# The reciprocals of the softmax sums take a way through DRAM instead of TensorE, and the gated products start a step later

## The chip, the core and the metric

The kernel runs on one core of a Trainium2 chip. A time is the device time of one execution in microseconds. Of the kernel before there are three runs, with the median 1103.42 us (1102.9 to 1108.34), and one profiled execution. In the profile PE is TensorE's matmul stream, DVE is VectorE, ACT is ScalarE, POOL is GpSimd, and SP is SyncE, which here issues nearly all DMAs.

## What is computed

An attention with a threshold, a gated feed-forward network and a second feed-forward network, all in float32:

```python
scores = scale * q @ k.T                              # 4 batches, 8 heads, 576 tokens, 64 wide
scores = where(scores >= max(scores) - tau, scores, -1e9)
attn = exp(scores - max(scores))
attn = attn / (attn.sum(-1) + 1e-9)
x = (attn @ v)                                        # heads side by side: 2304 tokens x 512
h = ((x @ w1) * (x @ w2)) @ w3 @ w_out                # 1024 wide inside
out = leaky_relu(h @ w_in, 0.01) @ w_out2             # 2048 wide inside
```

The change concerns the division by the sum: one factor for each query of each head.

## The kernel before

**Units and steps.** A unit is a pair of heads and one of two groups of queries. There are 32. Group 0 has 256 queries, in two chunks of 128 (a "two-chunk unit", two steps); group 1 has 320, in a chunk of 64 queries that carries both heads side by side on the partitions (`None` in the code) and two chunks of 128 (a "three-chunk unit", three steps). For each batch the four pairs of group 0 come first and then the four of group 1, so four two-chunk units (8 steps) and four three-chunk units (12 steps) alternate, and there are 80 steps.

**One step.** In step n the loop (lines 455 to 516 of before) masks chunk n, issues the scores of chunk n + 1, transposes the masked exponentials of chunk n, and in the first step of a unit multiplies the unit before with its values (`weighted`, tile `av`, copied to `xs`). Scores (`sc`, L219; L215 for the `None` chunk) stand in one PSUM tile with a single buffer. VectorE takes the maximum of each head (`nm`, L225), ScalarE the exponential (`e`, L227), and VectorE masks it and sums it (L241). In the last step of a unit VectorE also scales the next unit's queries (`qk`, L199), and for a three-chunk unit copies the 64-query part, scaled, into a block-diagonal tile `qz` (L194), which the next L215 reads.

**The sums.** VectorE makes the reciprocals `rr` (L305, L306), one row per query on 128 partitions. The heads' outputs `xs` have queries along the free axis and 64 partitions per head, so each reciprocal is needed on 64 partitions. Before, GpSimd spreads it (`rb`, L308 and L313), TensorE transposes it into PSUM (`bc`, L324; L322 for the chunk of 64), and VectorE multiplies (L325). This is `normalise`. ScalarE and GpSimd then split the product into two parts, `x`.

**The filler.** When the four units of a group are done, their `x` go through the gated network (`gated`): 24 pieces of 12 matmuls each (tiles `psab`, L383, and `psh`, L402), which the loop deals out between the scores and the transposes of the next group's steps. How many a step gets follows from a running sum: rate 1.22 or 1.55 times the step's weight (1 for the `None` chunk, 2 for others), rounded down, the rest carried on; a step's pieces stand at three places. Until the first gated pass the filler is the product of two weight matrices (`fold_weights`, L361), whose operands ScalarE, VectorE and GpSimd decode from 64-bit words (L142 to L153).

**What sets the order.** PE's order in the attention is the order of the code (`manual_schedule`). SyncE's too, until the second gated pass begins; after that, and on the other engines, a scheduler sets it, except that instructions marked `keep_in_program_order` keep their order among each other. `av`, `bc`, `psab`, `psh` and the fold share two PSUM buffers (tag `w`).

Of the kernel before, what the change touches and what calls it, by code (L numbers as in the profile page):

```python
# [8 lines left out]
F32 = mybir.dt.float32  # L9
# [4 lines left out]
ALU = mybir.AluOpType  # L14
# [3 lines left out]
P = 128  # L18
B, H, S, D = 4, 8, 576, 64
# [9 lines left out]
Q0 = (0, 128, 320, 448)  # L29
GROUPS = ((0, 256, (0, 1)), (HF, 320, (2, 3)))  # L30
NK = 5
CHUNKS = ((0, 1), (None, 2, 3))
STEPS = tuple(
    (b * 4 + p, g, c) for b in range(B) for g in range(2) for p in range(4) for c in CHUNKS[g])
# [5 lines left out]
def attention_gated_ffn(ctx: ExitStack, tc: tile.TileContext, qkv, tau, w3t, wout, w12, w2, out):  # L40
# [6 lines left out]
    nc = tc.nc  # L47
# [8 lines left out]
    h3d = tc.dram_tile([KD, P, NT], F32, name="h3d")  # L56

# [10 lines left out]
    pairs = cpool.tile([P, D], F32, name="pairs")  # L68
    nc.vector.tensor_tensor(out=pairs, in0=ident[:, :D], in1=ident[:, D:], op=ALU.add)
    sides = cpool.tile([P, P], F32, name="sides")  # L70
    nc.vector.memset(sides, 0.0)
    nc.vector.memset(sides[:D, :D], 1.0)
    nc.vector.memset(sides[D:, D:], 1.0)
# [4 lines left out]
    one = cpool.tile([P, 1], F32, name="one")  # L78
    nc.vector.memset(one, 1.0)
# [220 lines left out]
    def reciprocals(pair, g):  # L300

        st = stat.pop((pair, g))
        n = 4 + g
        rr = apool.tile([P, 5], F32, tag="rr", name="rr", bufs=2)
        nc.vector.tensor_scalar(out=rr[:, :n], in0=st[:, :n], scalar1=1e-9, scalar2=None, op0=ALU.add)  # L305
        nc.vector.reciprocal(rr[:, :n], rr[:, :n])  # L306
        rb = apool.tile([P, 3, P], F32, tag="rb", name="rb")
        nc.gpsimd.tensor_tensor(  # L308
            out=rb[:, :2].rearrange("p c (h d) -> p (c h) d", h=2),
            in0=rr[:, :4].unsqueeze(2).to_broadcast([P, 4, D]),  # L310
            in1=one.unsqueeze(2).to_broadcast([P, 4, D]), op=ALU.mult)
        if g:
            nc.gpsimd.tensor_tensor(  # L313
                out=rb[:, 2], in0=rr[:, 4:5].to_broadcast([P, P]), in1=sides, op=ALU.mult)
        rb_t[pair, g] = rb

    def normalise(pair, g):
        gq, gw, cs = GROUPS[g]
        xs, rb = xs_t.pop((pair, g)), rb_t.pop((pair, g))
        bc = ps_w.tile([P, 512], F32, tag="w", name="bc")  # L320
        if g:
            nc.tensor.matmul(bc[:, :D], rb[:, 2], pairs, start=True, stop=True)  # L322
        for i, c in enumerate(cs):
            nc.tensor.transpose(bc[:, Q0[c] - gq:Q0[c] - gq + P], rb[:, i], ident)  # L324
        nc.vector.tensor_tensor(out=xs[:, :gw], in0=xs[:, :gw], in1=bc[:, :gw], op=ALU.mult)  # L325
        x = xpool.tile([P, 2, 320], F32R, tag="x", name="x")
        nc.scalar.copy(x[:, 0, :gw], xs[:, :gw])
        nc.gpsimd.tensor_tensor(
            out=x[:, 1, :gw], in0=xs[:, :gw], in1=f(x[:, 0, :gw]), op=ALU.subtract)
        x_t[pair, g] = x  # L330
# [106 lines left out]
    def run(gen, k):  # L437
        for _ in range(k):
            if next(gen, 0) == 0:
                return  # L440
# [10 lines left out]
    weigh, norm = [], []  # L451
# [3 lines left out]
    for n in range(NS):  # L455
# [30 lines left out]
        if norm:  # L486
            normalise(*norm.pop())
        if last_of_unit:
            reciprocals(pair, g)
            weigh.append((pair, g))  # L490
        elif u and STEPS[n - 1][:2] != (pair, g):
            norm.append(units[u - 1])
        fill(2)
        if n == 0 or STEPS[n - 1][:2] != (pair, g):
            load_unit(u + 2)
        load_halves(kh - kh // 2)
        if last_of_unit and pair % 4 == 3:
            queue.append((n + 2, pair // 4, g))
# [18 lines left out]
    weighted(*weigh.pop())  # L517
    run(filler, 2)
# [140 lines left out]
```

## Time and profile before

| | us |
|---|---|
| median of three runs | 1103.42 |
| profiled execution | 1105.57 |
| its span, first to last instruction | 1103.8 |
| PE busy | 1054.0 |
| VectorE busy | 508.8 |
| ScalarE busy | 473.5 |
| GpSimd busy | 256.6 |

The span is 1.77 us shorter than the execution that it is from, and that execution 2.15 us longer than the median. Attention fills the first 650 us, the rest is the second network. "Granted clock" is TensorE's clock as a share of 2.4 GHz; its lower level, 0.50, is 1.2 GHz. A matmul's own duration in the profile includes its way through the array, so that neighbours overlap: what one adds is read from the starts.

### The profile page before, as it was taken

To read this page: it belongs to the slowest core of one execution; us is meant where nothing else is said; L and a number is where in the kernel's file an instruction comes from. 1 tells how busy PE (TensorE), PEld (TensorE's weight loads), DVE (VectorE), ACT (ScalarE), POOL (GpSimd) and SP (SyncE) were. 2 spreads that over 40 slices of the span, in tenths; PEclk is the share of its full clock that TensorE was granted. 3 is DMA by queue.
4 is the path that set the end of the run, shared out by engine and by line. 5 is a ranking of instruction groups with operands and counts; after the bars stand their busy time and mean duration, and the time that the engine had idled before them with its cause. 6 is when DMAs were issued, how large, how long until landed. Compare 5 with 4: busy or idle time off the path is not lost.

```text
span 1103.8 us, 16025 instructions
## 1 busy us (share of the span) xinstructions
PE 1054.0 (95%) x6288; PEld 852.2 (77%) x6288; DVE 508.8 (46%) x1087; ACT 473.5 (43%) x891; POOL 256.6 (23%) x256
## 2 busy tenths in 40 slices
PE   4799799999999999999999999999999999999998
PEld 2455478788877798887888789877888888888887
DVE  5666767555665555675546633365311211111111
ACT  4667744343444343543434443477422222222232
POOL 2436812021120111120212136477400100000000
PEclk8899899999999999999999999999999999999999
DMA  9563720311112111112120023356200010010010
GB/s 306 185 210 117 211 59 19 85 30 58 53 35 66 50 41 54 55 38 66 34 65 25 1 77 116 101 191 197 71 18 1 31 37 1 3 45 1 1 39 20
DMA packets 35098, 77.57 MB, mean 70 GB/s; under 512 B 4560, under 2 KB 19408, under 8 KB 32976
## 3 DMA queue, kind: packets, MB, share of 16 engines
q1 hardware_dynamic: 34880, 76.56, 22.0%
q8 instruction: 49, 0.80, 0.3%
q14 instruction: 25, 0.20, 0.1%
q10 hardware_dynamic: 144, 0.00, 0.0%
HBM read 67.11 MB, written 9.44 MB: 69 GB/s over the span
## 4 chain that ended last, share of the span: by engine, by line
PE 81%; DVE 7%; ACT 6%; DMA 2%; issue 2%; POOL 1%; ACTq 0%; SPq 0%; DVEq 0%; POOLq 0%
PE psab L383 16%; PE po L596 16%; PE ps L574 16%; PE psh L402 9%; PE av L294 7%; PE sc L219 6%; PE tp L272 4%; PE ps L361 4%; DVE e L241 2%; DVE t L145 1%; ACT t L142 1%; ACT e L227 1%; PE tq L277 1%; ACT HH L276 1%; ACT lw L144 1%
## 5 line engine op out<-in xcount | busy, mean ns | idle before, releaser
L383 PE MATMUL psab<-x,w 128*128 128x256 f32 (+1 forms) x1536 | 234.2, 303 | 2.7 <-DVE xs L325 2.0
L383 PEld LDWEIGHTS psab<-x,w 128*128 128x128 f32 x1536 | 208.9, 189 | 24.3 <-issue 16.0
L574 PE MATMUL ps<-h,w 128*128 128x512 f32 (+1 forms) x960 | 215.7, 370 | 0.6 <-DVE h L550 0.3
L596 PE MATMUL po<-w,gg 128*128 128x512 f32 x864 | 213.7, 392 | 1.8 <-ACT gg L581 1.8
L574 PEld LDWEIGHTS ps<-h,w 128*128 128x128 f32 x960 | 169.0, 188 | 36.5 <-POOL w L153 1.3
L596 PEld LDWEIGHTS po<-w,gg 128*128 128x128 f32 x864 | 159.3, 188 | 38.0 <-ACT gg L581 3.1
L582 DVE TENSOR_TENSOR gg<-gf,gg 128x512 fp32r<-128x512 f32 (+1 forms) x80 | 61.2, 765 | 269.9 <-ACT gg L581 268.2
L225 DVE TENSOR_REDUCE nm<-sc 128x1 f32<-128x576 f32 x144 | 108.8, 756 | 109.2 <-PE sc L219 67.0
L227 ACT ACTIVATE e<-sc,nm 128x576 f32<-128x576 f32 x144 | 107.0, 743 | 121.0 <-DVE nm L225 120.8
L579 ACT ACTIVATE gf<-ps 128x512 f32<-128x512 f32 (+1 forms) x80 | 44.3, 555 | 226.9 <-PE ps L574 226.9
L241 DVE SCALAR_TENSOR_TENSOR e<-sc,th,e 128x576 f32<-128x576 f32 x144 | 112.6, 815 | 45.9 <-ACT e L227 45.9
L402 PE MATMUL psh<-gt,w 128*128 128x256 f32 (+1 forms) x768 | 115.1, 301 | 0.6 <-ACT ht L409 0.5
L394 POOL TENSOR_TENSOR gt<-at,gt 128x256 fp32r<-128x256 f32 (+1 forms) x64 | 52.7, 824 | 262.9 <-ACT gt L393 262.9
L402 PEld LDWEIGHTS psh<-gt,w 128*128 128x128 f32 x768 | 104.1, 189 | 7.7 <-issue 5.4
L219 PE MATMUL sc<-qk 64*128 64x288 f32 x512 | 84.7, 451 | 24.5 <-DVE e L241 15.7
L272 PE MATMUL tp<-ident,e 128*128 128x128 f32 x512 | 78.7, 277 | 9.0 <-ACT HH L276 9.0
L219 PEld LDWEIGHTS sc<-qk 64*128 64x128 f32 x512 | 46.7, 196 | 44.4 <-issue 12.6
L272 PEld LDWEIGHTS tp<-ident,e 128*128 128x128 f32 x512 | 61.5, 142 | 19.4 <-ACT HH L276 11.5
L151 POOL TENSOR_TENSOR lw<-t,lw 128x512 int32<-128x512 int32 x48 | 65.8, 1375 | 26.7 <-ACT lw L144 14.8
L294 PE MATMUL av<-HH,vv 128*64 128x256 f32 (+1 forms) x512 | 69.7, 415 | 0.0
L551 POOL TENSOR_TENSOR h<-hr,h 128x1024 fp32r<-128x1024 f32 (+1 forms) x10 | 23.8, 2380 | 188.1 <-DVE h L550 188.1
L361 PE MATMUL ps<-wo,w 128*128 128x512 f32 x128 | 60.9, 621 | 6.2 <-DVE xs L325 4.7
(70 smaller groups left out, 961.1 us busy)
## 6 DMA issues: line engine op xcount, KB each, us to landing
st<-in_w SPq DMA_DIRECT2D x40, 512.0 KB, 4.5
vv<-in_qkv SPq DMA_DIRECT2D x64, 160.0 KB, 2.4
raw<-in_w3t SPq DMA_DIRECT2D x8, 1024.0 KB, 5.6
qk<-in_qkv SPq DMA_DIRECT2D x32, 208.0 KB, 3.5
qk<-in_qkv SPq DMA_DIRECT2D x32, 144.0 KB, 2.8
out<-os SPq DMA_DIRECT2D x18, 256.0 KB, 2.2
raw<-in_wout SPq DMA_DIRECT2D x4, 1024.0 KB, 10.0
raw<-in_w SPq DMA_DIRECT2D x4, 1024.0 KB, 6.2
```

Source lines behind the costliest of these rows:

```text
L151: nc.gpsimd.tensor_tensor(out=lw, in0=t, in1=lw, op=ALU.add)
L219: nc.tensor.matmul(sc[:, a, half, :HS], qk[r, o:o + P], qk[r, ks], start=True, stop=True)
L225: nc.vector.tensor_reduce(out=nm, in_=sc[:, a, :, :HS], op=ALU.max, axis=AX.XY, negate=True)
L227: nc.scalar.activation(e[:, a].rearrange("p (a b) -> p a b", a=2), sc[:, a, :, :HS], AF.Exp, bias=nm)
L241: nc.vector.scalar_tensor_tensor(out=ev, in0=sc[:, a, :, :HS], scalar=th, in1=ev, op0=ALU.is_ge, op1=ALU.mult, accum_out=stat[key][:, o:o ...
L272: nc.tensor.transpose(tp[:, kc], e[:, a, kc * P:kc * P + P], ident)
L294: nc.tensor.matmul(av[a * D:a * D + D, :gw], vv[:, a, kc], rhs, start=(i == 0), stop=(i == NK - 1))
L361: nc.tensor.matmul(ps, w3_t[i][:, j * P:j * P + P], wo_t[j // 2][:, (j % 2) * 512:(j % 2) * 512 + 512], start=(j == 0), stop=(j == KF - 1))
L383: nc.tensor.matmul(ps[:, :gw], w12_t[i][:, a, mat * 512 + kk * P:mat * 512 + kk * P + P], xt[kk][:, c, :gw], start=(m == 0), stop=(m == 11))
L402: nc.tensor.matmul(ps[:, :gw], w34_t[i // 2][:, a, i % 2, o * P:o * P + P], gt[i][:, c, :gw], start=(m == 0), stop=(m == 23))
L574: nc.tensor.matmul(ps[:, :tw], w2_t[j][:, a, kk * P:kk * P + P], h3_t[ci][:, c, kk, :tw], start=(m == 0), stop=(m == 11))
L596: nc.tensor.matmul(po_t[t], gg[:, c, t * P:t * P + P], w2_t[j][:, a, 512:], start=(j == 0 and (a, c) == PASSES[0]), stop=(j == KF2 - 1 and ...
```

## The change

The reciprocals are stored to a DRAM tile `rd`, laid out per unit and head with the queries in a row (one 4-byte element from each partition), and loaded back from there with one row broadcast to the 64 partitions of a head (`spread`, into an SBUF tile `rb`). `reciprocals` issues the stores in the last step of a unit; `spread` is called one step later; `normalise`, now without matmuls, multiplies from SBUF three steps after the unit's last instead of two, and the product is marked to keep its order on VectorE. The gated pass of a group begins three steps after its last instead of two. The tiles that only the old way needed go.

```diff
@@ -54,6 +54,7 @@
     wld = ctx.enter_context(tc.tile_pool(name="wld", bufs=1))
     ps_w = ctx.enter_context(tc.tile_pool(name="ps_w", bufs=2, space=PSUM))
     h3d = tc.dram_tile([KD, P, NT], F32, name="h3d")
+    rd = tc.dram_tile([2 * B * 4, 2, 320], F32, name="rd")
 
     s_ffn = ExitStack()
     s_att = ExitStack()
@@ -65,18 +66,10 @@
 
     ident = cpool.tile([P, P], F32, name="ident")
     make_identity(nc, ident)
-    pairs = cpool.tile([P, D], F32, name="pairs")
-    nc.vector.tensor_tensor(out=pairs, in0=ident[:, :D], in1=ident[:, D:], op=ALU.add)
-    sides = cpool.tile([P, P], F32, name="sides")
-    nc.vector.memset(sides, 0.0)
-    nc.vector.memset(sides[:D, :D], 1.0)
-    nc.vector.memset(sides[D:, D:], 1.0)
     qz = [cpool.tile([P, P], F32, name=f"qz{i}") for i in range(2)]
     tl = [apool.tile([P, 2, 320], F32, name=f"tl{i}") for i in range(2)]
     for t in (*qz, *tl):
         nc.vector.memset(t, 0.0)
-    one = cpool.tile([P, 1], F32, name="one")
-    nc.vector.memset(one, 1.0)
     tauc = cpool.tile([P, 1], F32, name="tauc")
     neg = cpool.tile([P, 1], F32, name="neg")
     scl = cpool.tile([P, 1], F32, name="scl")
@@ -299,30 +292,32 @@
 
     def reciprocals(pair, g):
 
+        u = units.index((pair, g))
         st = stat.pop((pair, g))
-        n = 4 + g
+        gw, n, o = GROUPS[g][1], 4 + g, D * g
         rr = apool.tile([P, 5], F32, tag="rr", name="rr", bufs=2)
         nc.vector.tensor_scalar(out=rr[:, :n], in0=st[:, :n], scalar1=1e-9, scalar2=None, op0=ALU.add)
         nc.vector.reciprocal(rr[:, :n], rr[:, :n])
-        rb = apool.tile([P, 3, P], F32, tag="rb", name="rb")
-        nc.gpsimd.tensor_tensor(
-            out=rb[:, :2].rearrange("p c (h d) -> p (c h) d", h=2),
-            in0=rr[:, :4].unsqueeze(2).to_broadcast([P, 4, D]),
-            in1=one.unsqueeze(2).to_broadcast([P, 4, D]), op=ALU.mult)
-        if g:
-            nc.gpsimd.tensor_tensor(
-                out=rb[:, 2], in0=rr[:, 4:5].to_broadcast([P, P]), in1=sides, op=ALU.mult)
+        with nc.allow_non_contiguous_dma("sums of a chunk stand on partitions"):
+            for a in range(2):
+                nc.sync.dma_start(
+                    out=rd[u, a, o:o + 2 * P].rearrange("(c p) -> p c", p=P),
+                    in_=rr[:, :4].rearrange("p (c a) -> p c a", a=2)[:, :, a])
+            for a in range(2 * g):
+                nc.sync.dma_start(out=rd[u, a, :D].unsqueeze(1), in_=rr[a * D:a * D + D, 4:5])
+
+    def spread(pair, g):
+        u, gw = units.index((pair, g)), GROUPS[g][1]
+        rb = apool.tile([P, 320], F32, tag="rb", name="rb", bufs=2)
+        for a in range(2):
+            nc.sync.dma_start(out=rb[a * D:a * D + D, :gw], in_=rd[u, a:a + 1, :gw].to_broadcast([D, gw]))
         rb_t[pair, g] = rb
 
     def normalise(pair, g):
-        gq, gw, cs = GROUPS[g]
+        gw = GROUPS[g][1]
         xs, rb = xs_t.pop((pair, g)), rb_t.pop((pair, g))
-        bc = ps_w.tile([P, 512], F32, tag="w", name="bc")
-        if g:
-            nc.tensor.matmul(bc[:, :D], rb[:, 2], pairs, start=True, stop=True)
-        for i, c in enumerate(cs):
-            nc.tensor.transpose(bc[:, Q0[c] - gq:Q0[c] - gq + P], rb[:, i], ident)
-        nc.vector.tensor_tensor(out=xs[:, :gw], in0=xs[:, :gw], in1=bc[:, :gw], op=ALU.mult)
+        tc.keep_in_program_order(
+            nc.vector.tensor_tensor(out=xs[:, :gw], in0=xs[:, :gw], in1=rb[:, :gw], op=ALU.mult))
         x = xpool.tile([P, 2, 320], F32R, tag="x", name="x")
         nc.scalar.copy(x[:, 0, :gw], xs[:, :gw])
         nc.gpsimd.tensor_tensor(
@@ -448,7 +443,7 @@
 
     folding = fold_weights()
     scores(0)
-    weigh, norm = [], []
+    weigh, norm = [], {}
     filler = iter(())
     queue = []
     rate, due = 0.0, 0.0
@@ -483,19 +478,20 @@
         fill(1)
         for _ in pieces:
             pass
-        if norm:
-            normalise(*norm.pop())
+        if n in norm:
+            normalise(*norm.pop(n))
         if last_of_unit:
             reciprocals(pair, g)
             weigh.append((pair, g))
-        elif u and STEPS[n - 1][:2] != (pair, g):
-            norm.append(units[u - 1])
+            norm[n + 3] = (pair, g)
         fill(2)
         if n == 0 or STEPS[n - 1][:2] != (pair, g):
+            if u:
+                spread(*units[u - 1])
             load_unit(u + 2)
         load_halves(kh - kh // 2)
         if last_of_unit and pair % 4 == 3:
-            queue.append((n + 2, pair // 4, g))
+            queue.append((n + 3, pair // 4, g))
         if queue and queue[0][0] == n:
             _, b, gg = queue.pop(0)
             while halves_in[0] < 26:
@@ -515,6 +511,7 @@
             filler = gated(b, gg)
             rate, due = (1.22, 1.55)[gg], 0.0
     weighted(*weigh.pop())
+    spread(B * 4 - 1, 1)
     run(filler, 2)
     normalise(B * 4 - 1, 1)
     pe_order.close()```

PE's order, in a three-chunk unit while a gated pass runs: from the scores of the unit's last chunk (L219, in after L212) to the first scores of the next unit (L215, in after L208). `tp` and `tq` are the transposes, `psab` is a gated piece. Before:

```order
L219 MATMUL sc<-qk 128x288 x4
L383 MATMUL psab<-x,w_737 128x256 x12
L272 MATMUL tp<-ident,e 128x128 x4
L277 MATMUL tq<-ident,e 128x128
L383 MATMUL psab<-x,w_810 128x256 x12
L272 MATMUL tp<-ident,e 128x128 x4
L277 MATMUL tq<-ident,e 128x128
L322 MATMUL bc<-pairs,rb 128x64
L324 MATMUL bc<-ident,rb 128x128 x2
L383 MATMUL psab<-x,w_810 128x256 x12
L215 MATMUL sc<-qk,qz_93 128x288 x2
```

The same stretch of the same unit after:

```order
L212 MATMUL sc<-qk 128x288 x4
L378 MATMUL psab<-x,w_714 128x256 x12
L265 MATMUL tp<-ident,e 128x128 x4
L270 MATMUL tq<-ident,e 128x128
L378 MATMUL psab<-x,w_733 128x256 x12
L265 MATMUL tp<-ident,e 128x128 x4
L270 MATMUL tq<-ident,e 128x128
L208 MATMUL sc<-qk,qz_88 128x288 x2
```

The `bc` rows are gone, and of three gated pieces two are left between the two scores.

PE's order at the end of a group of three-chunk units, when a gated pass runs out: the two scores (L219) of the second two-chunk unit and what lies between them. `psh` rows of 6 make a piece two by two. Before:

```order
L219 MATMUL sc<-qk 128x288 x4
L402 MATMUL psh<-gt,w_768 128x256 x6
L402 MATMUL psh<-gt,w_968 128x256 x6
L272 MATMUL tp<-ident,e 128x128 x4
L277 MATMUL tq<-ident,e 128x128
L272 MATMUL tp<-ident,e 128x128 x4
L277 MATMUL tq<-ident,e 128x128
L322 MATMUL bc<-pairs,rb 128x64
L324 MATMUL bc<-ident,rb 128x128 x2
L219 MATMUL sc<-qk 128x288 x4
```

After, the same two scores:

```order
L212 MATMUL sc<-qk 128x288 x4
L397 MATMUL psh<-gt,w_391 128x256 x6
L397 MATMUL psh<-gt,w_578 128x256 x6
L265 MATMUL tp<-ident,e 128x128 x4
L270 MATMUL tq<-ident,e 128x128
L397 MATMUL psh<-gt,w_764 128x256 x6
L397 MATMUL psh<-gt,w_964 128x256 x6
L265 MATMUL tp<-ident,e 128x128 x4
L270 MATMUL tq<-ident,e 128x128
L397 MATMUL psh<-gt,w_391 128x256 x6
L397 MATMUL psh<-gt,w_578 128x256 x6
L212 MATMUL sc<-qk 128x288 x4
```

Where one piece stood there are now three, and the transposes without a piece between them come one stretch later.

SyncE's order in a stretch of two units, loads of a coming unit. Before (`vv`, `qk`):

```order
L181 DMA vv<-in_qkv 128x320 x2
L176 DMA qk<-in_qkv 64x832 x2
L181 DMA vv<-in_qkv 128x320 x2
L176 DMA qk<-in_qkv 64x832 x2
L181 DMA vv<-in_qkv 128x320 x2
```

After, with the stores (`rd`) and the broadcast loads (`rb`):

```order
L174 DMA vv<-in_qkv 128x320 x2
L169 DMA qk<-in_qkv 64x832 x2
L303 DMA rd<-rr 128x2x1 x2
L307 DMA rd<-rr 64x1 x2
L313 DMA rb<-rd 64x320 x2
L174 DMA vv<-in_qkv 128x320 x2
L169 DMA qk<-in_qkv 64x832 x2
```

Six DMAs a three-chunk unit and four a two-chunk unit have come between the loads.

## Rows read from the trace of the kernel before

**Rows 1.** The page: busy time of the engines, and shares of the chain that ended last.

```profile
PE 1054.0 (95%) x6288; PEld 852.2 (77%) x6288; DVE 508.8 (46%) x1087; ACT 473.5 (43%) x891; POOL 256.6 (23%) x256
...
PE 81%; DVE 7%; ACT 6%; DMA 2%; issue 2%; POOL 1%; ACTq 0%; SPq 0%; DVEq 0%; POOLq 0%
```

**Rows 2.** Busy time by stage: length, busy us (instructions) per engine, granted clock, DMA share, GB/s.

```profile
250.00:650.00 400.00, 391.18 (x2895) 330.64 (x2892) 234.20 (x577) 171.77 (x339) 66.70 (x96) 1.00 0.15 45
```

**Rows 3.** PE in order of time: start, length, what, count, in brackets idle before.

```profile
306.35 1.24 PE L219 MATMUL sc<-qk 64*128 64x288 f32 x8
...
312.54 1.24 PE L219 MATMUL sc<-qk 64*128 64x288 f32 x8
...
315.68 0.27 PE L277 MATMUL tq<-ident,e 128*128 128x128 f32 x1
315.70 1.67 PE L383 MATMUL psab<-x,w 128*128 128x256 f32 x12
...
317.65 0.27 PE L277 MATMUL tq<-ident,e 128*128 128x128 f32 x1
...
318.07 1.67 PE L383 MATMUL psab<-x,w 128*128 128x256 f32 x12
319.58 1.17 PE L215 MATMUL sc<-qk,qz 128*128 128x288 f32 x4
...
325.16 1.24 PE L219 MATMUL sc<-qk 64*128 64x288 f32 x8
```

**Rows 4.** PE in order of time, the end of a step of a two-chunk unit.

```profile
378.66 0.27 PE L277 MATMUL tq<-ident,e 128*128 128x128 f32 x1
...
378.96 2.03 PE L383 MATMUL psab<-x,w 128*128 128x320 f32 x12
```

**Rows 5.** VectorE in order of time, the stretch of rows 3.

```profile
313.83 0.76 DVE L225 TENSOR_REDUCE nm<-sc 128x1 f32<-128x576 f32 x1 [0.88 <-PE sc L219]
...
318.93 0.53 DVE L194 TENSOR_SCALAR qz<-qk,scl 64x64 f32<-64x64 f32 x2
```

**Rows 6.** PE's waits from 125 to 650 us: us in all, times, longest.

```profile
PE psab L383 <- DVE xs L325: 2.0, 8, 0.3
```

**Rows 7.** PE in order of time, the end of a three-chunk group.

```profile
344.71 1.24 PE L219 MATMUL sc<-qk 64*128 64x288 f32 x8 [0.84 <-DVE e L241]
...
358.29 0.66 PE L272 MATMUL tp<-ident,e 128*128 128x128 f32 x4 [0.57 <-ACT HH L276]
...
361.20 2.29 PE L219 MATMUL sc<-qk 64*128 64x288 f32 x8 [1.75 <-DVE e L241]
```

**Rows 8.** Busy time by stretch, four stretches of the attention stage.

```profile
100.00:125.00 25.00, 18.12 (x51) 8.34 (x51) 21.10 (x35) 20.27 (x37) 20.02 (x17) 0.81 0.64 208
200.00:225.00 25.00, 22.68 (x159) 18.57 (x158) 12.06 (x28) 8.79 (x17) 2.36 (x3) 0.93 0.33 90
350.00:400.00 50.00, 47.68 (x340) 40.65 (x338) 27.13 (x66) 20.32 (x41) 8.52 (x11) 0.97 0.15 44
500.00:550.00 50.00, 47.68 (x352) 41.16 (x348) 28.16 (x69) 21.37 (x43) 8.53 (x11) 1.00 0.16 46
```

**Rows 9.** PE in order of time, around the first gated start.

```profile
114.49 0.66 PE L272 MATMUL tp<-ident,e 128*128 128x128 f32 x4 [2.17 <-ACT HH L276]
...
120.18 9.86 PE L361 MATMUL ps<-wo,w 128*128 128x512 f32 x16 [4.71 <-DVE xs L325]
```

**Rows 10.** ScalarE in order of time, around the first gated start.

```profile
126.65 0.62 ACT L150 CAST w<-t 128x512 fp32r<-128x512 f32 x1 [1.54 <-PE ps L361]
```

**Rows 11.** DMA issues: what, count, KB each, median us to landing.

```profile
vv<-in_qkv SPq DMA_DIRECT2D x64, 160.0 KB, 2.4
...
h3d<-ht SPq DMA_DIRECT2D x16, 128.0 KB, 1.7
```

**Rows 12.** SyncE's waits, whole span: us in all, times, longest.

```profile
SPq L410 <- ACT ht L409: 164.1, 30, 20.2
```

## Prediction

> **What bounds the kernel now.** I read the busy shares first, then the chain that ended last, then PE's busy time stage by stage. PE is busy 1054.0 of 1103.8 us and holds 81% of the chain [rows 1]; from 250 to 650 us, where attention and the first feed-forward products run together, it is busy 391.18 of 400 us [rows 2]. In that stage PE's order is written out, so the time is PE's own work plus the few places where the next instruction in that order is not ready. The change touches both: it takes work off PE, and it shifts the pieces of gated product that lie between the scores. So I read next what stands between one chunk's scores and the next [rows 3] and what VectorE does in the same stretch [rows 5]. The scores live in one PSUM tile, so the next scores wait until the mask of the last has read it; the first scores of a unit also wait for its scaled queries (qz), which VectorE makes right after that mask.
>
> **What goes from PE.** In a three-chunk unit the gap from tq to the next gated piece is 317.65 to 318.07, 0.42 us, with the bc matmuls in it, and 315.68 to 315.70, 0.02, without [rows 3]: 0.40 us a unit, 16 units, 6.4 us. In a two-chunk unit it is 378.66 to 378.96, 0.30 us [rows 4], less the same 0.02 to 0.03: 0.27 us, 16 units, 4.3 us. (The rows' own durations overlap and would count too much.) Together -10.7 us, nearly all of it where PE is the bound. The bc tile also sat in one of the two PSUM buffers of the products, and PE waited eight times, 2.0 us in all, for the product to empty it [rows 6]: -2.0.
>
> **What the later gated start moves.** A gated pass has 24 pieces, dealt out by a running sum over the steps. Starting one step later, it meets the steps in another phase. The order shows it: between the scores of a three-chunk unit's last chunk and the first scores of the next unit, before has three L383 pieces and the bc matmuls, after only two pieces; the third piece falls behind the next unit's first scores. In the trace this stretch runs from 312.54 to 319.58, 7.04 us [rows 3]. Without one piece (318.07 to 319.58, 1.51) and the bc (0.40) PE would be through in 5.1 us. But qz ends at 318.93 + 0.53 = 319.46 [rows 5], 6.92 after the scores began, so with the usual 0.06 of a semaphore the next scores cannot begin before 6.98. VectorE's chain there (maximum, exponential on ScalarE, second maximum, two masks, qz) has nothing in it that the change takes away. PE therefore waits about 1.8 us at each such place. Going through PE's order there are 11 of them (in each of the first three three-chunk groups three, in the last two): +19.8 us. The stretch after it (319.58 to 325.16) only gets the piece as added work; its single-head chain is short, and the extra cover is wasted there.
>
> The same shift helps at the other end of a three-chunk group. There before has too few pieces: waits of 0.84, 0.57 and 1.75 us [rows 7], in three groups. After, the order puts one more piece between the scores of the first of these stretches and two more in the other. The 0.84 and the 1.75 go; the two transpose groups without a piece between them, which cost the 0.57, only move one stretch on, and with the VectorE chain there I leave 0.9 of waiting. So 3 x (3.16 - 0.9) = -6.8. In two of these three places the granted clock then fell: it is 0.93 in 200 to 225 and 0.97 in 350 to 400, but 1.00 in 500 to 550 [rows 8]; 25 x 0.07 and 50 x 0.03 give about 1.6 us of full-speed work lost each time: -3.3.
>
> **The first gated start.** Around 112 to 126 us PE waits 2.17 us for a copy and 4.71 for the product that empties bc [rows 9]. The second goes, but its place is taken at once: VectorE was late (25 us with 21.10 busy) and ScalarE full (20.27 busy) with decoding weights [rows 8], and ScalarE itself waited for the last fold to free a buffer [rows 10]. After, the fold is spread into the following step, its PE time there covers ScalarE's decoding, and the scores come before it. In ScalarE's new order the rest of the decoding stands ahead of the second chunk's exponentials, so I let attention there win about 5 us, bounded by the ScalarE waits that can go; of these 3.4 are two gated pieces (1.51 each) and a bc that PE has not done yet and does later. Net -1.7, between 0 and -7.
>
> **The way through DRAM.** Per unit it adds two to four small stores and two broadcast loads on SyncE's queue. No row shows a store of 4-byte elements; the nearest are the 128 KB stores of ht, 1.7 us to landing [rows 11]. The load is issued a step after the store and the product stands two steps after that: 7.04 + 5.58 us or more, less 1.51 and 0.40 but with the new wait, some 12 us of cover for the load. I take 0. It cannot go below: a transfer gives back no PE time that is not counted already. Above, the load alone would have to take five times the 2.4 us of the vv loads [rows 11] to reach the product on a free queue, and the store has a step of its own before that. What could do it is SyncE itself, which has waited up to 20.2 us in front of one store [rows 12]. VectorE's product costs what it did, 0.4 to 0.5 us, in SBUF instead of PSUM; now pinned, it stands in the slack of a unit's first chunk. GpSimd loses 48 broadcasts; at 23% busy [rows 1] that is worth nothing: 0.
>
> The Trainium skill (DMA: Bandwidth & Descriptors, Specifications) says that transfers below 512 B are handled by read-modify-write and miss line rate, which speaks against 4-byte elements; it gives no time for one, and none of these rows has one. By it the stores are slower than the rows of ht suggest, and the sum stays as it is until they eat the 12 us.
>
> **The sum.** -10.7 - 2.0 + 19.8 - 6.8 - 3.3 - 1.7 = -4.7. Left is what the new waits do to the clock. After the waits of 0.57 and 1.75 it fell in two of three places [rows 7, 8]. A new wait of 1.8 is about as long as the longest of these. If three or so of the eleven are followed by the low clock, at 1.6 us each, that gives back +5. The sum is then +0.3, which is nothing. The profiled execution took 1105.57 us (span 1103.8), 2.15 above the median of the runs, 1103.42; the difference applies to both alike, so I forecast 1103.5. What can be told from no change is about 0.5%, 5.5 us.
>
> **The rivals.**
> - The new waits come, the clock holds: no +5, and the first gated start wins all its 7 us: 1103.4 - 4.7 - 5.3, about 1093. For it: in the third place, 500 to 550, the same waits lowered nothing [rows 8]. Against: in two they did. Chance 0.19.
> - VectorE is not as late as I read it, and PE simply loses its work and its waits: without the +19.8 and the +5 that follows, 1103.4 - 24.5 = 1079. Against it stands qz in its row: it ended 0.12 us before the scores that needed it. Chance 0.06.
> - Slower by the clock: each of the new waits is followed by the low clock, since they recur in every unit: 11 x 1.6 = 17.6, so 1103.4 - 4.7 + 17.6 = 1116. It decides the sign from the sixth or seventh place on (6.5 x 1.6 = 10.4, less 4.7, is the 5.5 that can be told). Chance 0.15.
> - Slower by the queue: a store of h3d or a load that waits for PE stands on SyncE ahead of the broadcast, rb is late, and VectorE, in order, stops at the product with masks and copies queued behind it, for which PE waits. Each us beyond the cover costs a us; 2 us in 12 of the units is +24, 1127. It begins when queue and load take over 12 us. Before's longest wait of 20.2 us speaks for it, that SyncE had nothing else due in that wait speaks against. Chance 0.10.
>
> **The numbers.** My forecast, within 5.5 us either side, has 0.50; its own range is 1098 to 1109. Faster: 0.19 + 0.06 = 0.25. Slower: 0.15 + 0.10 = 0.25. For 8 in 10 the range takes in the clock both ways and leaves out the 1079 and the late queue: 1092 to 1116.
>
> **What would show it.** Right: no bc on PE; PE's wait for qz (L215's scores) appears in eight places and for the scaled queries in three, each near 1.8 us; the waits of 0.84 and 1.75 at the end of a three-chunk group are gone; a three-chunk unit takes about 1.2 us longer than its 18.81 (306.35 to 325.16 [rows 3]), a two-chunk group is shorter; VectorE does not wait for rb. Wrong: no waits for qz (then near 1080), PEclk below 1.0 in most slices from 130 to 650 us (then over 1110), or VectorE idle before the product for a DMA.

## The result, and the profile after

| | before | after |
|---|---|---|
| median of the runs beside each other, us | 1104.55 (1102.9 to 1108.34, 6 runs) | 1114.43 (1112.16 to 1116.99, 6 runs) |
| profiled execution, us | 1105.57 | 1112.16 |
| its span, us | 1103.8 | 1110.4 |

The ratio after/before is 1.0078, 95% interval 1.0059 to 1.0096: the change makes the kernel slower, by 8.6 us on 1104.5. I had forecast 1103.5, no change, with its own range 1098 to 1109 and a wider one of 1092 to 1116: the time lies outside the first and inside the second. Differences between experiments below are differences of such ratios, times 1104.5. The interval of one ratio is 1.6 to 3.4 us either side (5.4 for the run without the pin), so a difference of two is good to 3 or 4 us.

The page after, engines' busy time and shares of the chain that ended last, against [rows 1]:

```profile
PE 1045.1 (94%) x6192; PEld 846.2 (76%) x6192; DVE 509.4 (46%) x1082; ACT 473.1 (43%) x891; POOL 231.6 (21%) x208
...
PE 79%; ACT 7%; DVE 5%; DMA 5%; issue 2%; POOL 1%; SPq 0%; ACTq 0%; DVEq 0%; POOLq 0%
```

PE is busy 8.9 us less and the span is 6.6 longer, so PE stands idle 15.5 us more. DMA's share of the chain has gone from 2% to 5%. The stretches of after that answer to [rows 2, 8] (busy us per engine in the order PE, PEld, DVE, ACT, POOL; then granted clock, DMA share, GB/s):

```profile
100.00:125.00 25.00, 16.14 (x47) 8.16 (x46) 17.28 (x33) 15.77 (x30) 16.05 (x13) 0.81 0.74 171
200.00:225.00 25.00, 24.38 (x189) 19.28 (x188) 15.82 (x39) 10.88 (x21) 1.75 (x2) 1.00 0.24 61
250.00:650.00 400.00, 385.57 (x2849) 327.02 (x2846) 237.15 (x580) 172.75 (x342) 52.79 (x66) 1.00 0.23 52
350.00:400.00 50.00, 49.38 (x372) 40.89 (x369) 30.57 (x73) 22.29 (x44) 5.70 (x7) 1.00 0.31 73
```

Three things are to be seen. The clock is 1.00 wherever it had been 0.93 or 0.97. PE is fuller at the ends of the three-chunk groups (200 to 225, 350 to 400), but less full over the whole stage, 385.57 against 391.18. And in 100 to 125 all of PE, VectorE and ScalarE have less to do while the DMA share is higher and the bandwidth lower: 0.74 for 171 GB/s, where before 0.64 gave 208.

**The steady stage.** PE's waits from 125 to 650 us (us in all, times, longest), against [rows 6, 7]:

```profile
PE sc L208 <- DVE qz L187: 12.8, 8, 1.6
PE sc L212 <- DVE qk L192: 4.2, 3, 1.4
PE sc L212 <- DVE e L234: 4.2, 1, 4.2
```

These are the forecast eleven waits, 8 and 3, of 1.6 and 1.4 in place of 1.8. (The 4.2 for the mask, `e`, is a single wait, at the first gated start.) The psab waits for the product are gone, and so are the 0.84 and 1.75. The stretch of [rows 3] after, from the scores of the last chunk to those that wait for qz:

```profile
315.20 1.24 PE L212 MATMUL sc<-qk 64*128 64x288 f32 x8
316.37 1.69 PE L378 MATMUL psab<-x,w 128*128 128x256 f32 x12
...
318.37 1.67 PE L378 MATMUL psab<-x,w 128*128 128x256 f32 x12
...
320.31 0.27 PE L270 MATMUL tq<-ident,e 128*128 128x128 f32 x1
322.15 1.24 PE L208 MATMUL sc<-qk,qz 128*128 128x288 f32 x4 [1.57 <-DVE qz L187]
```

From scores to scores 6.95 us, where the prediction had 6.98 from VectorE's chain alone [rows 5].

**The first gated start.** The chain of after around 101 us (start, length, what), and ScalarE's and PE's rows that hang on it, against [rows 9, 10]:

```profile
100.89 11.57 DMA raw<-in_w
112.56 0.66 ACT t L135
```

```profile
112.56 0.66 ACT L135 ACTIVATE t<-raw 128x512 f32<-128x512 f32 x1 [6.28 <-DMA raw<-in_w]
```

```profile
119.69 1.11 PE L265 MATMUL tp<-ident,e 128*128 128x128 f32 x4 [8.10 <-ACT HH L269]
```

A load of weights (`raw`, 1 MB) takes 11.57 us; ScalarE, which decodes it, waits 6.28; PE, whose transposes need a copy that ScalarE makes afterwards, waits 8.10. The DMA groups after (KB each, median us from issue to landing), against [rows 11]:

```profile
vv<-in_qkv SPq DMA_DIRECT2D x64, 160.0 KB, 2.7
raw<-in_w3t SPq DMA_DIRECT2D x8, 1024.0 KB, 9.2
...
raw<-in_w SPq DMA_DIRECT2D x4, 1024.0 KB, 9.5
...
rb<-rd SPq DMA_DIRECT2D x32, 64.0 KB, 3.7
...
rd<-rr SPq DMA_DIRECT2D x64, 1.0 KB, 8.1
rd<-rr SPq DMA_DIRECT2D x32, 0.2 KB, 7.6
```

and of before, the same weight loads, not shown so far:

```profile
raw<-in_w3t SPq DMA_DIRECT2D x8, 1024.0 KB, 5.6
...
raw<-in_w SPq DMA_DIRECT2D x4, 1024.0 KB, 6.2
```

A store of 1 KB in 4-byte elements takes 8.1 us to land, longer than a load of 1 MB took before, and the 1 MB loads now take 9.2 to 9.5.

**The last unit.** Its stores and its load on SyncE, the product on VectorE, two copies on ScalarE, and PE:

```profile
640.45 0.88 SPq L303 DMA_DIRECT2D rd<-rr  x2
641.38 1.11 SPq L307 DMA_DIRECT2D rd<-rr  x2
649.99 1.10 SPq L313 DMA_DIRECT2D rb<-rd  x2
```

```profile
653.44 0.49 DVE L320 TENSOR_TENSOR xs<-xs,rb 128x320 f32<-128x320 f32 x1 [9.69 <-DMA rb<-rd]
```

```profile
653.96 0.46 ACT L322 CAST x<-xs 128x320 fp32r<-128x320 f32 x1 [6.48 <-DVE xs L320]
...
656.21 0.37 ACT L404 COPY ht<-psh 128x256 f32<-128x256 f32 x1
```

```profile
646.94 6.01 PE L397 MATMUL psh<-gt,w 128*128 128x256 f32 x48
656.62 5.38 PE L397 MATMUL psh<-gt,w 128*128 128x256 f32 x24 [3.67 <-ACT ht L404]
```

SyncE issues the load only when the stores have landed, at 649.99; VectorE stands 9.69 us before the product; ScalarE is behind it with the copy of x, and the copy of `ht` that PE needs for a free buffer stands behind that. PE then runs 24 matmuls in 5.38 us, where it had run 48 in 6.01 just before: the granted clock is 0.52 from 656.6 to 662.0, near the lower level.

**Where the time is lost.** The scores of steps 13 and 79 cut the span in three. Before:

```profile
142.22 1.24 PE L219 MATMUL sc<-qk 64*128 64x288 f32 x8 [1.02 <-DVE e L241]
...
632.72 1.24 PE L219 MATMUL sc<-qk 64*128 64x288 f32 x8
```

After:

```profile
144.30 2.29 PE L212 MATMUL sc<-qk 64*128 64x288 f32 x8 [4.17 <-DVE e L234]
...
632.85 1.24 PE L212 MATMUL sc<-qk 64*128 64x288 f32 x8
```

From step 13 to 79 it is 490.50 us before and 488.55 after; the loss lies outside, 2.1 us before step 13 and 6.5 after step 79 (471.08 and 477.55 to the end of the span). The middle has as many gated pieces before as after. The later start moves two of them: PE has done one of the first pass at step 13 instead of three, and has eleven of the seventh left after the scores of step 79 instead of nine. Readings from step 13 to 79 agree within 0.3 us (488.55, 488.32 and 488.34 in three kernels below that have the same order there); step 13 itself does not repeat so well, it comes at 144.30 to 147.20 us in four kernels with the same order on PE up to it.

So there were three suspects for the 8.6 us: the eleven waits, the stores at the first gated start, the last unit. The rival to the second is the later start itself.

### The profile page after: what moved, and what is told of

The parts are those of the page before. It is cut to its first block, busy times and chain, and to the rows that moved or that the text cites. A ratio compares the mean times of both kernels' runs of the same rounds, so it can differ in the third digit from the quotient of the medians.

```text
span 1110.4 us, 16011 instructions
## 1 busy us (share of the span) xinstructions
PE 1045.1 (94%) x6192; PEld 846.2 (76%) x6192; DVE 509.4 (46%) x1082; ACT 473.1 (43%) x891; POOL 231.6 (21%) x208
## 4 chain that ended last, share of the span: by engine, by line
PE 79%; ACT 7%; DVE 5%; DMA 5%; issue 2%; POOL 1%; SPq 0%; ACTq 0%; DVEq 0%; POOLq 0%
PE psab L378 17%; PE ps L571 16%; PE po L593 16%; PE psh L397 8%; PE sc L212 6%; PE av L287 6%; PE tp L265 4%; PE ps L356 3%; DVE e L234 2%; DMA st<-in_w 2%; ACT e L220 2%; PE sc L208 1%; ACT t L135 1%; DMA rd<-rr 1%; DVE t L138 1%
## 5 line engine op out<-in xcount | busy, mean ns | idle before, releaser
L378 PE MATMUL psab<-x,w 128*128 128x256 f32 (+1 forms) x1536 | 235.9, 304 | 0.0
L378 PEld LDWEIGHTS psab<-x,w 128*128 128x128 f32 x1536 | 210.4, 190 | 19.6 <-issue 11.9
L234 DVE SCALAR_TENSOR_TENSOR e<-sc,th,e 128x576 f32<-128x576 f32 x144 | 112.5, 815 | 46.4 <-ACT e L220 46.4
L397 PE MATMUL psh<-gt,w 128*128 128x256 f32 (+1 forms) x768 | 117.3, 306 | 3.7 <-ACT ht L404 3.7
L397 PEld LDWEIGHTS psh<-gt,w 128*128 128x128 f32 x768 | 106.5, 193 | 9.6 <-issue 5.4
L212 PE MATMUL sc<-qk 64*128 64x288 f32 x512 | 84.7, 452 | 24.1 <-DVE qk L192 13.0
L265 PE MATMUL tp<-ident,e 128*128 128x128 f32 x512 | 79.5, 279 | 15.6 <-ACT HH L269 15.3
L265 PEld LDWEIGHTS tp<-ident,e 128*128 128x128 f32 x512 | 62.2, 143 | 27.7 <-ACT HH L269 18.1
L212 PEld LDWEIGHTS sc<-qk 64*128 64x128 f32 x512 | 46.7, 196 | 43.5 <-issue 14.3
L138 DVE TENSOR_SCALAR t<-t 128x512 int32<-128x512 int32 x72 | 50.3, 702 | 33.3 <-ACT t L135 33.1
L267 DVE COPY HH<-tp 128x512 f32<-128x512 f32 x64 | 44.0, 687 | 44.6 <-PE tp L265 44.4
## 6 DMA issues: line engine op xcount, KB each, us to landing
raw<-in_w3t SPq DMA_DIRECT2D x8, 1024.0 KB, 9.2
raw<-in_wout SPq DMA_DIRECT2D x4, 1024.0 KB, 10.1
raw<-in_w SPq DMA_DIRECT2D x4, 1024.0 KB, 9.5
```

The costliest lines, as they stand in the source:

```text
L138: nc.vector.tensor_scalar(out=t, in0=t, scalar1=3, scalar2=None, op0=ALU.logical_shift_left)
L212: nc.tensor.matmul(sc[:, a, half, :HS], qk[r, o:o + P], qk[r, ks], start=True, stop=True)
L234: nc.vector.scalar_tensor_tensor(out=ev, in0=sc[:, a, :, :HS], scalar=th, in1=ev, op0=ALU.is_ge, op1=ALU.mult, accum_out=stat[key][:, o:o ...
L265: nc.tensor.transpose(tp[:, kc], e[:, a, kc * P:kc * P + P], ident)
L378: nc.tensor.matmul(ps[:, :gw], w12_t[i][:, a, mat * 512 + kk * P:mat * 512 + kk * P + P], xt[kk][:, c, :gw], start=(m == 0), stop=(m == 11))
L397: nc.tensor.matmul(ps[:, :gw], w34_t[i // 2][:, a, i % 2, o * P:o * P + P], gt[i][:, c, :gw], start=(m == 0), stop=(m == 23))
```

## The experiments

**Pieces in the old phase.** The pass still starts a step later, but its running sum starts where before's stood by then (2 x 1.22, less the whole pieces: 0.44).

```diff
-            rate, due = (1.22, 1.55)[gg], 0.0
+            rate, due = (1.22, 1.55)[gg], (0.44, 0.0)[gg]
```

> The changed kernel, but the running sum that deals out the gated pieces starts each pass over a two-chunk group's output at 0.44 instead of 0, so that the pieces meet the steps in the phase that they had before, while the pass still begins a step later. Theory (the shift of phase makes the eleven waits for qz and the scaled queries): they go, 8 x 1.6 + 3 x 1.4 = 17 us, 1114.4 - 17 = about 1097.5. Rival (VectorE's pinned product or the way through DRAM is what makes VectorE late, and the phase only shows it): the waits stay, 1114. Second rival (the waits go, but the waits of 0.84 and 1.75 at the end of a three-chunk group come back): 1097.5 + 7 = about 1104.5.

Measured: 1107.65, ratio 1.0020 (1.0002 to 1.0038), 6.4 us less than the changed kernel. PE's waits from 125 to 650 us:

```profile
PE sc L212 <- DVE e L234: 10.1, 7, 5.1
...
PE sc L208 <- DVE qz L187: 0.8, 4, 0.2
```

The waits for qz fell from 12.8 to 0.8 and those for the scaled queries went: the phase makes them, not the pinned product. But the time is nearer to the second rival: six waits of 0.82 to 0.84 (of the 10.1; the seventh, 5.1, is at the first gated start) stand at the ends of the three-chunk groups, where before had three of 0.84 and three of 1.75. From the scores of step 13 to those of step 79 this kernel takes 479.4 us (146.79 to 626.21) and the changed one 488.6 (144.30 to 632.85): the phase is worth 9.1 there. That is more than the 6.4 of the whole time, but within its uncertainty; the 2.5 us by which this run comes later to step 13 say nothing, since the order on PE up to there is the same.

**The last unit, and the first four units, the old way.** Two runs with one edit and two conditions: `u == 31` in the first, `u < 4` in the second. (`one` is a column of ones. `spread` returns at once for these units. The last unit's chunk of 64 goes through the free tile `qz[0]`, whose other blocks are zero, and two small matmuls.)

```diff
+        if u == 31:
+            rb = apool.tile([P, 320], F32, tag="rb", name="rb", bufs=2)
+            wide = rr[:, :4].unsqueeze(2).to_broadcast([P, 4, D])
+            nc.gpsimd.tensor_tensor(
+                out=rb[:, :256].rearrange("p (k d) -> p k d", d=D), in0=wide, in1=one.unsqueeze(2).to_broadcast([P, 4, D]), op=ALU.mult)
...
+            rb_t[pair, g] = rb
+            return
...
+        if u == 31:
+            bc = ps_w.tile([P, 512], F32, tag="w", name="bc")
...
+            for i, c in enumerate(cs):
+                nc.tensor.transpose(bc[:, Q0[c] - gq:Q0[c] - gq + P], rb[:, i * P:i * P + P], ident)
+            rb = bc
         tc.keep_in_program_order(
```

> The changed kernel, but the last unit's reciprocals go the old way: GpSimd spreads them, TensorE transposes them, VectorE multiplies from PSUM. Theory (in the last unit nothing covers the way through DRAM: VectorE waits 9.7 us for rb, ScalarE's copy of x stands ahead of a copy of ht, and PE waits 3.67 us and runs at the low clock behind it): the wait and the low clock go, about -6, 1108.5. Rival (the end is late because the later start left two more gated pieces for it, whichever way the reciprocals take): 1113 to 1114.

Measured: 1110.91, ratio 1.0043 (1.0028 to 1.0058), 3.9 less than the changed kernel. The way through DRAM in the last unit costs that. It is less than the 6 expected: PE's wait of 3.67 goes, and the clock is 1.00 from 652 to 664, but a wait of 1.4 for decoded weights and one of 0.7 for a gated copy come in its place. From the scores of step 79 to the end this kernel takes 473.7 us, the changed one 477.6 and the one before 471.1; so the rival holds for the other 2.6, with two more pieces there. They are moved work, not added work: as many fewer stand before step 13.

> The changed kernel, but the first four units, which are done before the first gated pass begins, take the old way (GpSimd and TensorE); the later start stays. Theory (the stores of 4-byte elements share the DMA queues with the loads of weights, and SyncE waits for them before it issues the load behind them: the load that took 11.57 us instead of 4.85 held ScalarE and then PE): the waits of 6.3 on ScalarE and 8.1 on PE near 113 to 120 us shrink to those of before, 5 to 9 us less, about 1105.5 to 1109.5. Rival (the later start itself makes this stretch longer): 1113 to 1114.5.

Measured: 1104.78, ratio 0.9994 (0.9978 to 1.0010), 9.3 less than the changed kernel, from four units of 32. The stretch 100 to 125 of this run, and its weight loads:

```profile
100.00:125.00 25.00, 22.60 (x71) 11.29 (x70) 22.70 (x40) 21.01 (x39) 19.56 (x16) 0.93 0.72 217
```

```profile
raw<-in_w3t SPq DMA_DIRECT2D x8, 1024.0 KB, 5.6
...
raw<-in_w SPq DMA_DIRECT2D x4, 1024.0 KB, 6.4
```

The loads are back at 5.6 and 6.4, and PE is busy 22.60 of 25 us, against 16.14. The later start is here unchanged, so it is not what made this stretch long: with the old way in these units the scores of step 13 come at 138.43 (140.39 and 140.93 in two more kernels with this order up to there), against 142.22 before, which has done two more pieces by then, and 144.30 to 147.20 with the changed order. So some 6 of the 9.3 stand before step 13; where the rest is won no run shows, and 3 us are within the uncertainty.

**The stores alone, and stores of whole rows.** To the kernel before, the changed kernel's stores are added; nothing reads them. In a second run rr is stored as it stands, in rows of 16 or 20 bytes, by this line in place of those stores:

```diff
+        nc.sync.dma_start(out=rd[units.index((pair, g)), :, :n], in_=rr[:, :n])
```

> The kernel before with the stores of the changed one (4-byte elements from rr to DRAM) added as ballast: nothing reads them, nobody waits for them. Theory (they slow the loads of weights by sharing the DMA queues): +5 to +7, 1110 to 1112, all of it before 145 us, and nothing from there to 640 us. Rival (SyncE's own wait, in front of the broadcast load, for the store to land is what did the harm): no such wait here, 1105 to 1106.

> As the ballast of the run before it, but rr is stored as it stands, one store of 128 pieces of 16 or 20 bytes a unit in place of two to four stores of 512 to 640 pieces of 4 bytes. Theory (the number of pieces is what costs): a quarter of the ballast's loss, +1.5, about 1107. Rival (any small store at that time does it): the same as the ballast of single elements, 1110 to 1112.

Measured: 1111.44, ratio 1.0046 (1.0029 to 1.0063), for the 4-byte elements, +5.1; 1105.09, ratio 0.9990 (0.9975 to 1.0004), for the rows, no loss at all. The chain of the first, two weight loads in a row:

```profile
98.89 4.84 DMA raw<-in_w
...
105.60 9.27 DMA raw<-in_w
```

The DMA groups of the second:

```profile
rd<-rr SPq DMA_DIRECT2D x16, 2.0 KB, 1.8
rd<-rr SPq DMA_DIRECT2D x16, 2.5 KB, 1.5
```

One store of rows, 2 KB, lands in 1.8 us, where one of single elements, 1 KB, took 8.1 in the changed kernel. So it is not the bytes that cost. The number of pieces (128 for 512 in a two-chunk unit), the size of a piece and the number of stores changed together, and no run separates them; if it is the number of pieces, then not in proportion, since a quarter of them cost nothing, where the theory had a quarter of the loss. The whole loss of the first run stands early: the scores of step 13 come 6.0 later than before (148.26 against 142.22), those of step 79 5.95 (638.67 against 632.72). Of the two loads shown, the first was issued 0.43 us ahead of the stores of a unit and took 4.84, as before (4.85); the second was issued 6.3 us behind them and took 9.27. No broadcast load stands there for SyncE to stop at, and the 9.27 run from the load's own issue: the load is held in the queue, behind the stores. (SyncE shows 5.4 us of waits that end with these stores, at loads of the next weights, but later: the 6.0 are complete at the scores of step 11, 135.92 against 129.88.)

**The broadcast load a step later.**

```diff
-            if u:
-                spread(*units[u - 1])
             load_unit(u + 2)
+        if n - 1 in late:
+            spread(*late.pop(n - 1))
+        if u and (n == 0 or STEPS[n - 1][:2] != (pair, g)):
+            late[n] = units[u - 1]
```

(`late` is empty at the start.)

> The changed kernel with each broadcast load issued one step later, still a step ahead of the product, so that the stores have two steps to land before SyncE stops for them. Theory (the queues are shared, SyncE's wait is not the cause): 1112.5 to 1115. Rival (SyncE stands up to 11 us at the load with other loads behind it): its waits of 17 us in the first 140 us go and the time comes to 1105 to 1108. Third (the product comes to wait, since only one step is left for the load): over 1118.

Measured: 1116.44, ratio 1.0097 (1.0072 to 1.0122), 2.1 more than the changed kernel, which is within the uncertainty. SyncE's waits for the stores up to 140 us went down from 17.1 to 11.3 and nothing was won, which agrees with the run of the stores alone; since they did not go altogether, that run is the cleaner test. The product waits for rb three times now, 12.4 us in all, but 10.3 of them in the last unit, where the changed kernel waits 9.7; in the steady stage a single step of cover is short by 2.1 us in two places.

**The product without its pin.**

```diff
-        tc.keep_in_program_order(
-            nc.vector.tensor_tensor(out=xs[:, :gw], in0=xs[:, :gw], in1=rb[:, :gw], op=ALU.mult))
+        nc.vector.tensor_tensor(out=xs[:, :gw], in0=xs[:, :gw], in1=rb[:, :gw], op=ALU.mult)
```

> The changed kernel without the mark that keeps the product in VectorE's order. Theory (the pin costs nothing, VectorE has slack at that place, and the eleven waits come from the phase): 1113 to 1116, waits for qz and the scaled queries as before at 17 us. Rival (the pin holds masks and maxima back): under 1110, with the waits shorter.

Measured: 1137.06, ratio 1.0272 (1.0223 to 1.0320), 21.4 more than the changed kernel: neither side had it. VectorE's waits from 150 to 680 us, and one of them in order of time:

```profile
DVE xs L319 <- DMA rb<-rd: 27.7, 15, 4.2
```

```profile
239.38 0.43 DVE L319 TENSOR_TENSOR xs<-xs,rb 128x256 f32<-128x256 f32 x1 [4.23 <-DMA rb<-rd]
```

Left to the scheduler, the product stands earlier on VectorE, in 15 units before its data is there, and the next maximum stands behind it. The pin is what makes the cover through DRAM real.

**Only the later start, the old way everywhere.**

```diff
-            queue.append((n + 2, pair // 4, g))
+            queue.append((n + 3, pair // 4, g))
```

> The kernel before with only the later start of the gated pass, the old way of the reciprocals everywhere and the pieces dealt as in the changed kernel. Theory (the losses and gains add: 1114.4 less 9.3 and 3.9 for the stores and the last unit, plus 12.7 for bc): about 1112 to 1114, and the waits for qz and the scaled queries shorter by bc's 0.4 each at most. Rival (bc on PE only fills what would be a wait there, so the phase costs less with it): 1107 to 1109, as with the pieces in the old phase.

Measured: 1113.40, ratio 1.0074 (1.0048 to 1.0099), +8.2 against before. PE's waits from 125 to 650 us:

```profile
PE sc L215 <- DVE qz L194: 8.5, 7, 1.2
...
PE sc L219 <- DVE qk L199: 3.0, 3, 1.0
```

Ten of the eleven waits stand here, and each is shorter by the 0.4 of bc, which stands in front of it, as expected. Another has come that neither the kernel before nor the changed one has:

```profile
PE psab L383 <- DVE at L391: 4.1, 6, 0.7
```

Each stands right behind the bc matmuls, at a gated piece that waits for one of the two PSUM buffers which `bc` and `psab` share.

**The later start in the old phase, the old way everywhere.** Both one-line edits above, on the kernel before.

> The kernel before (reciprocals through GpSimd and TensorE everywhere) with the gated pass a step later and its pieces dealt in the old phase. It differs from the kernel of the last experiment mainly in bc, which 27 units there do without. Theory (bc on PE costs what its gaps show, 0.40 and 0.27 us a unit, and the psab waits 2.0 in all): 27 of 32 units are worth 10.7, so 1094.3 + 10.7 = about 1105, no change against before. Rival (bc stood where PE would have waited for VectorE anyway, and the later start alone brings the gain): 1096 to 1099.

Measured: 1108.21, ratio 1.0016 (1.0001 to 1.0032). Against the combined kernel below that is 12.7 us for bc and its waits in 27 units; from step 13 to step 79 the two take 490.0 us (139.79 to 629.82) and 478.3 (140.39 to 618.65), 11.8 apart. (A kernel with the same order as the combined one up to step 79, the last one below, takes 480.2, which makes it 9.8.) The theory had 10.7. But the six waits of 0.7 stand in this kernel too, 4.1 us, so it is the price of bc beside a later start, not that of bc in the kernel before. The later start alone brings no gain.

**All three together.**

> All three together: the pieces dealt in the old phase, the first four units and the last one the old way, DRAM for the other 27. If the three losses are separate and of the sizes above: 1114.4 - 17 - 6 - 7 = about 1084, 20 us faster than the kernel before. Rival (they cover each other, PE being late for one reason where the other is taken away): 1095 to 1104.

Measured: 1094.26, ratio 0.9901 (0.9870 to 0.9931): 19.5 less than the changed kernel, and the three single gains, 6.4 + 3.9 + 9.3, are 19.6. They add, as far as 4 us of uncertainty can tell. This kernel is 1% faster than the one before. Its page:

```profile
PE 1047.6 (96%) x6206; PEld 847.1 (77%) x6206; DVE 513.9 (47%) x1083; ACT 472.9 (43%) x891; POOL 234.7 (21%) x215
...
PE 81%; ACT 7%; DVE 6%; issue 3%; DMA 2%; POOL 1%; SPq 0%; ACTq 0%; DVEq 0%; POOLq 0%
```

DMA is back at 2% of the chain.

**More gated pieces ahead of the last product.** On the changed kernel, and on the combined one with the last unit through DRAM again.

```diff
-    run(filler, 2)
+    run(filler, 6)
```

> The changed kernel; at the end, six gated pieces in place of two are issued before the last product, so that the copies of ht stand ahead of the copy of x on ScalarE. Theory (the product's DRAM way is slow there, but the loss comes only from what is queued behind it): PE's wait of 3.67 us and the low clock go, 1108.5 to 1110.5. Rival (the last pass then waits for x instead): 1113 to 1115.

> Pieces dealt in the old phase, the first four units the old way, the last unit through DRAM but with six gated pieces issued ahead of its product. If the tail's loss is only what is queued behind the product, this is as fast as the version with the last unit the old way or a little faster, 1092 to 1095; if the way through DRAM still holds the last pass, 1096 to 1099.

Measured: 1114.66, ratio 1.0086 (1.0061 to 1.0111), and 1097.34, ratio 0.9934 (0.9908 to 0.9961). The first did not try what it was meant to: on ScalarE, where a scheduler sets the order, the copy of x still stands ahead of that of `ht`, and PE waits 3.9 us as it had.

```profile
656.56 0.46 ACT L322 CAST x<-xs 128x320 fp32r<-128x320 f32 x1 [6.73 <-DVE xs L320]
...
658.80 0.37 ACT L404 COPY ht<-psh 128x256 f32<-128x256 f32 x1
```

So its theory is neither shown nor refuted. In the second, too, PE waits 3.4 us for that copy. It is 3.6 us slower than the combined kernel (0.9934 less 0.9901), but this is no second measurement of the last unit's price: of the 4.0 between the two profiled spans 2.5 stand before step 79, where the order is the same, and 1.5 behind it.

## Why the prediction failed where it did

| step of the prediction | said | measured |
|---|---|---|
| steady stage, without the clock term (-10.7 - 2.0 + 19.8 - 6.8 - 3.3) | -3.0 | -2.0 from step 13 to 79 |
| of it, bc off PE and the psab waits | -12.7 | -12.7 (9.8 to 11.8 from step 13 to 79) in 27 units, of which 4.1 are not the kernel before's |
| phase and first gated start (+19.8 - 6.8 - 3.3 - 1.7) | +8.0 with bc gone | +8.2 with bc in place |
| low clock after the new waits | +5 | none |
| way through DRAM | 0 | +9.3 first units, +3.9 last unit |
| sum | +0.3 | the whole change, +8.6 |

The measured terms may not be added up. The +8.2 is from a kernel that keeps bc: there bc fills 0.4 of each wait, so the sum's own terms would give +3.6 for it, and the 4.1 of buffer waits, which the sum does not have, are most of the rest. The same 4.1 are in the -12.7. That two of these numbers equal what was said is luck; the first row is the like-for-like one.

**What held.** The mechanism of the steady stage, with its sizes: the order told how many waits there would be and VectorE's rows how long each, eleven, 1.6 and 1.4 instead of 1.8, so 17.0 instead of 19.8, and the stage as a whole came within about 1 us. The gain at the ends of the three-chunk groups is there (waits of 0.62 are left in three places, where I had left 0.9), and the old phase brings waits back. Without the stores, the first gated start comes to step 13 earlier by 1.3 to 3.8 us, where I had about 5; the two pieces not done then are done after step 79, where the later start with the old way takes 473.8 us (638.50 to the end) against 471.1. So its net is about 0, at the upper end of my 0 to -7.

**What failed: "The way through DRAM." "I take 0."** This term measured 13 us. The step asked only whether rb would be at the product in time. In the steady stage that was answered rightly: the product waits for rb once in the whole run, in the last unit, although SyncE stands behind its stores 38 times, 204 us in all. What it left out is what the stores do to others. In the first 130 us weights stream in, [rows 8] showed a DMA share of 0.64 there and ScalarE busy 20.27 of 25 us with decoding, and the stores went through the same queue. The load of 11.57 us was issued 4.6 us after the stores of a unit; in the run with the stores alone the load ahead of them took 4.84 and the one behind them 9.27. The Trainium skill (DMA: Bandwidth & Descriptors, Specifications), which I had cited, says that transfers below 512 B miss line rate; the trace agrees, 8.1 us for 1 KB, and I had let it count only for the product. The Trainium skill (DMA: Bandwidth & Descriptors, Queues, rings and completion order) says that each engine takes up the descriptors of a ring in their order; by that a load issued behind such stores starts behind them, and the two loads of that run agree. The lower bound of the step, no gain, agrees with the runs; the upper bound was worked out for one consumer only.

The second part of the failure is the last unit, where the cover is missing that the prediction had worked out for all units alike: its product comes right behind its last step. The rival "slower by the queue" described this mechanism (rb late, VectorE stopped, work queued behind it) but put it in twelve units at 2 us, where it stood in one at 3.9.

**The clock.** +5 was wrong: after each of the eleven waits of 1.4 to 1.6 us the granted clock stays at 1.00, in every stretch of 25 us from 150 to 650. It fell after the long waits, 8.10 us at the first gated start (0.81 in 100 to 125, as before) and 3.67 in the last unit (0.52). With this term the forecast came out 5 us higher for a reason that was not there, which hid 5 of the missing 13: that the time still lies in the wider range is partly luck.

**The pin** was costed at nothing, and nothing in the runs speaks against that. What the prediction did not see is that the change needs it: without it the product goes where its data is not, and 21.4 us more are lost.

## What to carry to other kernels

When a step puts small pieces on a DMA queue, ask not only whether its own data arrives in time but which other transfer is due behind it, and look first at the stretch with the highest DMA share. Cost the first and the last turn of a loop apart from the steady one: here five units of 32 lost 13 us, more than the 8.6 of the whole change, and undoing the change there, with the filler in its old phase, turned +0.8% into -1.0%. And where a scheduler sets the order, look whether it puts an instruction that waits for a transfer ahead of work that is ready; if it does, pin it behind.

## What the runs showed of the hardware

A store of 256 pieces of 4 bytes took 8.1 us (median) to land; one of 128 rows of 16 bytes, twice the bytes, 1.8. Loads of 1 MB that shared the queue went from 5.6 and 6.2 us to 9.2 and 9.5 with the first kind and stayed at 5.7 and 6.5 with the second. A load of 1 MB issued 0.4 us ahead of stores of the first kind took 4.84, one issued 6.3 us behind them 9.27. Eleven waits of 1.4 to 1.6 us on PE left its clock at the full level, though before it had fallen in two of three places around one of 1.75.
